# Issue order of the q, k and v loads around the DMA transposes, in a retention layer followed by a bilinear feed-forward layer

## The chip, the cores and the metric

The kernel runs on one core of one Trainium2 chip. The metric is the device time of one execution in microseconds, as the median of several runs. The engines are TensorE (PE in the profile, with its weight loads as PEld), VectorE (DVE), ScalarE (ACT), GpSimd (POOL) and SyncE (SP), which here only issues DMA transfers.

## What is computed

Four sequences of 768 steps, 8 heads of 64. Each head keeps a state of 64 x 64 that decays by a factor of its own; the output of that recurrence is the input x of a feed-forward layer with two products that are multiplied element by element.

```python
gamma = 1.0 - 2.0 ** (-5.0 - np.arange(H))
for t in range(S):
    state = gamma * state + einsum('bhd,bhe->bhde', k[:, :, t], v[:, :, t])
    y[:, :, t] = 1/sqrt(D) * einsum('bhd,bhde->bhe', q[:, :, t], state)
x = y.transpose(0, 2, 1, 3).reshape(3072, 512)
out = ((x @ w_a) * (x @ w_b)) @ w_out          # d_ff = 1536
```

## The kernel before

**Slots and blocks.** The 3072 rows are 24 slots of 128, six to a sequence; a sequence is worked on slot by slot, with the state carried along. The feed-forward layer runs over seven blocks of 4, 2, 2, 2, 2, 4 and 8 slots (`TILES`), named J = 0 to 6. While PE works on the feed-forward products of one block, the recurrence of the slots that come next is put between them (in block 3, slots 8 and 9, that of slots 10 to 13). The whole order is written out by hand at the end of the kernel (lines 888 to 1071), and `seq` chains the instructions of each engine in the order of the program, so no scheduler changes it.

**From load to scores.** Slots 0 to 5 are loaded in pairs and transposed on PE. From slot 6 on, a slot t goes this way:

1. SP loads k, q and v from DRAM (`load_slot`, lines 106 to 120). k and v come one slot at a time (256 KB each), into halves of a tile that two slots share. q comes for two slots at once (`load_two`, 512 KB), with the even one of them. The pool `raw` has three buffers for each of k, q and v.
2. POOL scales k and q with the decay tables into the bf16 tile `kqb` (`scaled`, line 283, 1.04 us each) and casts v (line 242); for slots 12 to 19, ACT casts v (`v_cast`).
3. SP issues a DMA transpose of `kqb` into `kqT` (`flip`, line 303). It waits for POOL's scaling of that slot.
4. PE reads `kqT` in `turn(new, old)` (lines 392 to 411): scores of the pair `new` (line 330), and output of the pair `old`. Scores of a slot need the transposes of both slots of its pair.

`casts(t)` (lines 290 to 298) does 2 and 3 for one slot and then issues the loads of slot t + 2. `casts_two(6)` (lines 307 to 315) does 2 and 3 for slots 6 and 7 and then issues the loads of slots 8 and 9 (`load_slots`).

**SP's queue.** SP works through its instructions in order; one that waits (a transpose for POOL, a store for its result) holds all behind it. The first loads of the program are a list, `LOADS` (line 21): pairs 0 and 1, weights, pair 2, output weights, and at its end `s6`, the loads of slots 6 and 7. All that is left of it after the first six entries is issued at line 923. Behind it come the transposes of 6 and 7, then the loads of 8 and 9, then for each slot its transpose and the loads of two slots later, with finished rows of the output (line 551) between them.

**Two slots that differ.** For t = 14 and t = 18 (`LATE_Q`, line 20), q is not issued with the even slot. It is issued at the head of the loads of slot 15 and slot 19, which stand in the queue behind the transposes of 13 and 17.

**Sums ahead of the products.** The output product of blocks 1 to 6 works with seven products in place of eight (`Group`, `single`), and needs sums and differences of parts of ht, the product of the two branches: tiles hs 1 to 4 (`hsum`, `hsums`, line 575). For blocks 2, 3 and 4, POOL makes them, between the casts: the difference hs 3 over all of ft 0 to 5, then hs 2, 1 and 4 in two halves, the first of which needs ft up to 8 and the second up to 11. In `single(J)`, PE uses hs 3 first, then hs 2, hs 1 and hs 4, with products of block J + 1 between them. In `big()` (block 6), POOL makes sums of the weights (`weight_pieces`) and then products into ht, which take part in the rotation of the buffers that DVE writes.

**Lines of the order that matter here.** `casts_two(6)` stands at line 981, `casts(8)` at 990, `casts(9)` at 998. `casts(12)` to `casts(14)` stand at 1009 to 1015 and `casts(16)` to `casts(18)` at 1030 to 1039, with `hsums(2, ...)`, `hsum(3, ...)`, `hsums(3, ...)` and `hsum(4, ...)` between them, all of them on POOL in that order.

Of the kernel before, what the change touches and what calls it, by code (L numbers as in the profile page):

```python
# [16 lines left out]
PAIRS = 3  # L17


LATE_Q = {14, 18}  # L20
LOADS = "p0 p1 w0 w1 a1 b1 a2 k2 q2 b2 v2 o0 o1 o2 o3 o4 o5 s6".split()


@with_exitstack
def kernel(
# [69 lines left out]
    def seq(bi):  # L95
        ins = bi.ins
        prev = last.get(ins.engine)
        if prev is not None:
            tc.add_manual_dep(ins, prev.name, nosync, reason="program order")
        last[ins.engine] = ins  # L100
        return bi
# [3 lines left out]

    def load_slot(t, names="kqv"):
        b, ci = divmod(t, NCH)
        if t - 1 in LATE_Q:
            load_two("q", q, b, ci // 2, t - 1)
        for nm in names:  # L110
            src = {"k": k, "q": q, "v": v}[nm]
            if nm == "q":
                if t % 2 == 0 and t not in LATE_Q:
                    load_two(nm, src, b, ci // 2, t)
                continue
            if t % 2 == 0:
                whole[nm] = raw.tile([P, 2, H, D], F32, tag=nm + "f", name=nm + "f")
            raws[nm, t] = whole[nm][:, t % 2]
            s = src[b, :, ci * P : (ci + 1) * P, :].rearrange("h p d -> p h d")
            seq(nc.sync.dma_start(out=raws[nm, t], in_=s))  # L120

    def load_slots(t):
        for u, names in ((t, "kq"), (t + 1, "k"), (t, "v"), (t + 1, "v")):
            load_slot(u, names)

    def load_two(nm, src, b, u, t):
        f = raw.tile([P, H, 2, D], F32, tag=nm + "f", name=nm + "f")
        s = src[b, :, 2 * u * P : 2 * (u + 1) * P, :].rearrange("h (p two) d -> p h two d", two=2)
        seq(nc.sync.dma_start(out=f, in_=s))  # L129
        for par in range(2):  # L130
            raws[nm, t + par] = f[:, :, par, :]
# [5 lines left out]
    def load_wide(nm, n):  # L137
        src = {"a": moe_w_a, "b": moe_w_b}[nm]
        for i in range(2):
            st = wstage.tile([P, 2, 2 * WC], F32, tag="w", name="wst" + nm)  # L140
            s = src[2 * i * P : 2 * (i + 1) * P, 2 * n * WC : 2 * (n + 1) * WC]
            seq(nc.sync.dma_start(out=st, in_=s.rearrange("(c p) f -> p c f", p=P)))
            wst[nm, n, i] = st
# [13 lines left out]

    pending = list(LOADS)

    def issue_loads(n):  # L160
        for _ in range(min(n, len(pending))):
            what = pending.pop(0)
            n = int(what[1:])
            if what[0] in "ab":
                load_wide(what[0], n)
            elif what[0] in "kqv":
                load_two(what[0], {"k": k, "q": q, "v": v}[what[0]], 0, n, 2 * n)
            else:
                {"p": load_pair, "s": load_slots, "w": load_w, "o": load_o}[what[0]](n)


    kqb = {}
    kqb = {}
    issue_loads(6)
    zero = osbp.tile([P, DM], F32, tag="osb", name="zero")
    seq(nc.vector.memset(zero, 0.0))
# [61 lines left out]
    def cast(engine, dst, src):  # L238
        if engine is nc.scalar:
            seq(nc.scalar.copy(dst, src))  # L240
        else:
            seq(engine.tensor_copy(dst, src))  # L242
# [29 lines left out]
    def scaled(eng, t, i):  # L272
        tab = tabs[0] if i else tabs[1 if t < 2 * PAIRS else 2]
        dst, src, tab = kqb[t][:, i], raws["kq"[i], t], tab[:, t % NCH]
        if t < 2 * PAIRS:
            dst, src = (x.rearrange("p (hp r) d -> p hp r d", r=2) if x is src else x
                        for x in (dst, src))
            tab = tab.rearrange("p (hp r) o -> p hp r o", r=2).to_broadcast([P, HP, 2, D])
        else:
            dst = dst.rearrange("p hp r d -> p r hp d")  # L280
            src = src.rearrange("p (r hp) d -> p r hp d", r=2)
            tab = tab.rearrange("p (r hp) o -> p r hp o", r=2).to_broadcast([P, 2, HP, D])
        seq(eng.tensor_tensor(dst, src, tab, op=ALU.mult))  # L283

    def new_nat(t):
        kqb[t] = nat.tile([P, 2, HP, 2, D], BF16, tag="kqb", name="kqb")
        kb[t], qb[t] = kqb[t][:, 0], kqb[t][:, 1]
        vb[t] = nat.tile([P, H, D], BF16, tag="vb", name="vb")

    def casts(t):  # L290
        new_nat(t)
        scaled(nc.gpsimd, t, 0)
        scaled(nc.gpsimd, t, 1)
        if t not in range(12, 20):
            cast(nc.gpsimd, vb[t], raws["v", t])
        flip(t)
        if t + 2 < NSLOT:
            load_slot(t + 2)

    def flip(t):  # L300
        if t % 2 == 0:
            kqT[t // 2] = tra.tile([P, 2, 2, HP, P], BF16, tag="kqT", name="kqT", bufs=3)
        seq(nc.sync.dma_start_transpose(
            out=kqT[t // 2][:, t % 2].rearrange("p a b c -> p (a b) c"),
            in_=kqb[t].rearrange("p a hp r d -> p (a hp r d)")))

    def casts_two(t):
        for u in (t, t + 1):
            new_nat(u)
            scaled(nc.gpsimd, u, 0)  # L310
            scaled(nc.gpsimd, u, 1)
            flip(u)
        for u in (t, t + 1):
            cast(nc.gpsimd, vb[u], raws["v", u])
        load_slots(t + 2)

    def half(i):
        return slice(64 * i, 64 * i + 64)
# [602 lines left out]
    update2(1, 1)  # L921
    ffn_g(0, 0, 0, W2)
    issue_loads(100)
    cast_w(1, parts=2)
    ffn_a(0, 0, W2, 2 * W2)
# [53 lines left out]
    for ft in range(NFT):  # L979
        ffn_ab(1, ft)  # L980
    casts_two(6)
    ffn_out(0, 0, 0)
    weight_sum(3)
# [118 lines left out]
```

## Time and profile before

| | |
|---|---|
| median of 3 runs | 222.21 us (222.01 to 222.92) |
| the profiled execution: its time | 222.79 us |
| the profiled execution: its span | 221.1 us |
| HBM read, written | 28.31 MB, 6.29 MB |
| share of the DMA engines taken by SP's queue | 75.8% |

The span is the time from the first to the last instruction that the profile shows. In a timeline, a row has the start in us, the duration in us, engine, line, operation and tiles, and the number of instructions that are merged into it; in brackets stands how long the engine was idle before it and what ended the idle time. On SP's queue (SPq) the duration is that of issuing a transfer, not of the transfer. A row of DMA issues has the tile, the count, the size and the median time from issue to landing.

### The profile page before, as it was taken

The numbers are of one execution on the slowest core, as the hardware profiler recorded it, in microseconds if no ns is written. First come the engines' busy times: TensorE is split into PE (matmuls) and PEld (weight loads), VectorE is DVE, ScalarE is ACT, GpSimd is POOL, SyncE is SP. The second block draws the span as 40 slices with busy tenths as digits, with TensorE's granted clock in tenths as the row PEclk, the third lists the DMA queues.
The fourth block names the chain that finished last, engine by engine and source line by source line (L and its number), as shares of the span: only waits on it lengthen the run. The fifth ranks groups of instructions, "written<-read, shape, count | busy, mean of one in ns | idle before, by whom it ended". The sixth has DMA issues, their size and how long they took to land.

```text
span 221.1 us, 5640 instructions
## 1 busy us (share of the span) xinstructions
PE 212.3 (96%) x2242; PEld 143.3 (65%) x2242; DVE 138.0 (62%) x254; ACT 99.3 (45%) x217; POOL 141.2 (64%) x163
## 2 busy tenths in 40 slices
PE   6789999999999999998999999999999999999994
PEld 2467445687468888887888565456865444448883
DVE  3776356846393463774377246986595777789642
ACT  3255325342243453453475345445545656542331
POOL 5265876775364659349782976999999996520000
PEclk9999999999999999999999999999999999999999
DMA  6999999998999999869999999990022000000054
GB/s 167 290 323 367 382 313 361 374 235 152 251 193 291 207 236 220 180 143 190 271 181 247 225 147 227 246 175 3 4 80 110 0 1 3 0 0 1 27 190 166
DMA packets 85146, 39.68 MB, mean 179 GB/s; under 512 B 57472, under 2 KB 78848, under 8 KB 85120
## 3 DMA queue, kind: packets, MB, share of 16 engines
q1 hardware_dynamic: 84976, 39.26, 75.8%
q8 instruction: 17, 0.28, 0.6%
q10 hardware_dynamic: 144, 0.07, 0.1%
q14 instruction: 9, 0.07, 0.1%
HBM read 28.31 MB, written 6.29 MB: 157 GB/s over the span
## 4 chain that ended last, share of the span: by engine, by line
PE 87%; SPq 4%; DMA 4%; POOL 2%; issue 1%; DVE 1%; ACT 0%; DVEq 0%
PE a L525 19%; PE g L537 18%; PE mA L641 12%; PE uA L781 8%; PE mB L641 6%; PE o L562 5%; PE uB L781 4%; DMA wstb<-in_moe_w_b_dram 4%; SPq L129 3%; PE mC L641 3%; PE at L330 2%; PE y L378 2%; PE uC L781 2%; PE st L348 2%; POOL hs L575 2%; PE ka L840 2%
## 5 line engine op out<-in xcount | busy, mean ns | idle before, releaser
L539 DVE TENSOR_TENSOR ht<-g,asb 128x256 bf16<-128x256 f32 (+1 forms) x74 | 36.9, 502 | 38.4 <-PE g L537 33.8
L525 PE MATMUL a<-xt,wa_bf 128*128 128x256 bf16 (+1 forms) x296 | 52.4, 305 | 0.2
L537 PE MATMUL g<-xt,wb_bf 128*128 128x256 bf16 (+1 forms) x296 | 52.2, 304 | 0.2 <-POOL wb_bf L242 0.2
L528 ACT CAST asb<-a 128x256 bf16<-128x256 f32 (+1 forms) x74 | 32.3, 437 | 39.0 <-PE a L525 36.6
L537 PEld LDWEIGHTS <-wb_bf 128*128 128x128 bf16 x296 | 28.6, 98 | 12.8 <-POOL wb_bf L242 0.3
L525 PEld LDWEIGHTS <-wa_bf 128*128 128x128 bf16 x296 | 27.9, 98 | 12.5 <-POOL wa_bf L242 0.4
L283 POOL TENSOR_TENSOR kqb<-kf,ktab 128x512 bf16<-128x512 f32 x22 | 23.0, 1051 | 16.6 <-DMA kf<-in_k_dram 14.9
L283 POOL TENSOR_TENSOR kqb<-qf,qtab 128x512 bf16<-128x512 f32 x18 | 19.0, 1053 | 12.8 <-DMA qf<-in_q_dram 12.8
L641 PEld LDWEIGHTS <-hs 128*128 128x128 bf16 x240 | 23.1, 98 | 5.6 <-POOL hs L575 1.7
L787 ACT COPY snap<-uA 128x512 f32<-128x512 f32 x30 | 16.7, 588 | 13.1 <-PE uA L781 13.1
L336 DVE TENSOR_TENSOR aT<-at,mask 128x512 bf16<-128x512 f32 x36 | 22.3, 681 | 0.3
L648 ACT COPY snaps<-mA 128x256 f32<-128x256 f32 x30 | 11.2, 374 | 21.2 <-PE mA L641 21.2
L641 PEld LDWEIGHTS <-ht 128*128 128x128 bf16 x180 | 17.5, 98 | 2.8
L575 POOL TENSOR_TENSOR hs<-ht,hs 128x384 bf16<-128x384 bf16 (+1 forms) x17 | 16.5, 982 | 2.5 <-DVE ht L539 2.5
L641 PE MATMUL mA<-wsum,hs 128*128 128x256 bf16 x120 | 16.1, 273 | 1.1 <-POOL hs L575 1.1
L575 POOL TENSOR_TENSOR ht<-gsb,asb 128x512 bf16<-128x512 bf16 x12 | 13.5, 1159 | 4.5 <-DVE gsb L575 4.5
L242 POOL CAST vb<-vf 128x512 bf16<-128x512 f32 x16 | 10.1, 645 | 8.4 <-DMA vf<-in_v_dram 8.2
L575 DVE TENSOR_TENSOR osb<-mB,snaps 128x256 f32<-128x256 f32 x20 | 8.4, 422 | 9.1 <-PE mB L641 4.7
L575 POOL TENSOR_TENSOR hs<-ht 128x384 bf16<-128x384 bf16 (+2 forms) x12 | 13.8, 1153 | 0.0
L389 ACT CAST xt<-y 128x512 bf16<-128x512 f32 x18 | 9.7, 589 | 2.3 <-PE y L378 2.2
L562 PE MATMUL o<-wo_bf,ht 128*128 128x512 bf16 x48 | 10.7, 379 | 0.0
L575 DVE TENSOR_TENSOR gsb<-uB,snap 128x512 bf16<-128x512 f32 x10 | 6.9, 685 | 5.4 <-ACT snap L787 2.6
(104 smaller groups left out, 325.9 us busy)
## 6 DMA issues: line engine op xcount, KB each, us to landing
qf<-in_q_dram SPq DMA_DIRECT2D x12, 512.0 KB, 5.9
out_dram<-osb SPq DMA_DIRECT2D x21, 256.0 KB, 4.2
kf<-in_k_dram SPq DMA_DIRECT2D x18, 256.0 KB, 4.6
vf<-in_v_dram SPq DMA_DIRECT2D x18, 256.0 KB, 5.3
wsta<-in_moe_w_a_dram SPq DMA_DIRECT2D x6, 512.0 KB, 7.9
wstb<-in_moe_w_b_dram SPq DMA_DIRECT2D x6, 512.0 KB, 8.2
wsto<-in_moe_w_out_dram SPq DMA_DIRECT2D x6, 512.0 KB, 8.7
kf<-in_k_dram SPq DMA_DIRECT2D x3, 512.0 KB, 7.2
```

The costliest lines, as they stand in the source:

```text
L283: seq(eng.tensor_tensor(dst, src, tab, op=ALU.mult))
L336: seq(nc.vector.tensor_tensor(aT[t][:, r], at[r], mask.to_broadcast([P, HP, P]), op=ALU.mult))
L525: seq(nc.tensor.matmul(a, wa_bf[:, kt, fs], xcols(J, kt, c0, c1), start=(kt == 0), stop=(kt == KT - 1)))
L528: seq(nc.scalar.copy(asb, a))
L537: seq(nc.tensor.matmul(g, wb_bf[:, kt, fs], xcols(J, kt, c0, c1), start=(kt == 0), stop=(kt == KT - 1)))
L539: seq(nc.vector.tensor_tensor(ht[J][:, ft, c0:c1], g, asbs.pop((J, ft, c0)), op=ALU.mult))
L562: seq(nc.tensor.matmul(o, ht[J][:, ft, i * P : (i + 1) * P], wo_bf[:, ft], start=(ft == 0), stop=(ft == NFT - 1), skip_group_check=True))
L575: seq(eng.tensor_tensor(dst, x, y, op=op))
L641: seq(nc.tensor.matmul(m, w, right[:, j], start=(first and j == 0), stop=(j == NP - 1), skip_group_check=True))
L648: seq(nc.scalar.copy(self.snaps[:, n], self.bank["A"]))
L781: seq(nc.tensor.matmul(m, w, right[:, k], start=(first and k == 0), stop=(k == 1), skip_group_check=True))
L787: seq(nc.scalar.copy(self.snaps[n], self.bank["A"]))
```

## The change

Three edits. `t8` is put at the end of `LOADS`: the loads of slot 8 (k, q of 8 and 9, v) are issued right behind those of slots 6 and 7, ahead of their transposes. `casts_two` issues the loads of slot 9 alone behind the transposes (k and v). `LATE_Q` goes: q of 14 and 15 is issued with slot 14 between its k and v, ahead of the transpose of 13, and q of 18 and 19 with slot 18, ahead of the transpose of 17. The instructions of PE, DVE, ACT and POOL are the same ones in the same order.

```diff
-LATE_Q = {14, 18}
-LOADS = "p0 p1 w0 w1 a1 b1 a2 k2 q2 b2 v2 o0 o1 o2 o3 o4 o5 s6".split()
+LOADS = "p0 p1 w0 w1 a1 b1 a2 k2 q2 b2 v2 o0 o1 o2 o3 o4 o5 s6 t8".split()
...
     def load_slot(t, names="kqv"):
         b, ci = divmod(t, NCH)
-        if t - 1 in LATE_Q:
-            load_two("q", q, b, ci // 2, t - 1)
         for nm in names:
             src = {"k": k, "q": q, "v": v}[nm]
             if nm == "q":
-                if t % 2 == 0 and t not in LATE_Q:
+                if t % 2 == 0:
                     load_two(nm, src, b, ci // 2, t)
                 continue
...
-                {"p": load_pair, "s": load_slots, "w": load_w, "o": load_o}[what[0]](n)
+                {"p": load_pair, "s": load_slots, "t": load_slot, "w": load_w, "o": load_o}[what[0]](n)
...
         for u in (t, t + 1):
             cast(nc.gpsimd, vb[u], raws["v", u])
-        load_slots(t + 2)
+        load_slot(t + 3)
```

## The prediction

> **What bounds the kernel now.** I read the page first, then the list of what TensorE waited for to find the places, then the timelines of PE, GpSimd (POOL), VectorE (DVE) and SyncE's queue (SP) around those waits, and last the landing time of single transfers.
>
> ```profile
> span 221.1 us, 5640 instructions
> ...
> PE 212.3 (96%) x2242; PEld 143.3 (65%) x2242; DVE 138.0 (62%) x254; ACT 99.3 (45%) x217; POOL 141.2 (64%) x163
> ```
>
> PE is busy for 212.3 of 221.1 us. A change that only moves loads can win nothing but PE's waits. What one costs is read from the starts of neighbouring groups on PE's timeline, since the pipeline has to fill again after a wait:
>
> ```profile
> 103.70 0.49 PE L641 MATMUL mA<-wsum,hs 128*128 128x256 bf16 x3
> 105.26 0.50 PE L641 MATMUL mA<-wsum,hs 128*128 128x256 bf16 x3 [1.07 <-POOL hs L575]
> 105.60 0.60 PE L525 MATMUL a<-xt,wa_bf 128*128 128x256 bf16 x4
> ...
> 106.47 0.82 PE L641 MATMUL mA<-wsum,hs 128*128 128x256 bf16 x6
> 107.13 0.60 PE L525 MATMUL a<-xt,wa_bf 128*128 128x256 bf16 x4
> ...
> 124.46 1.02 PE L641 MATMUL mA<-wsum,hs 128*128 128x256 bf16 x6
> 125.33 1.03 PE L525 MATMUL a<-xt,wa_bf 128*128 128x512 bf16 x4
> ```
>
> Six undisturbed mA matmuls take 107.13 - 106.47 = 0.66 us until the next group starts. In single(3) the six on hs 2 stop after three, until POOL's hs is there, and take 105.60 - 103.70 = 1.90: 1.24 us lost. In single(4) the same product takes 125.33 - 124.46 = 0.87: 0.21 lost. The third place is found in the chain of waits, in big():
>
> ```profile
> 173.96 0.86 PE uA L781 x4
> ...
> 176.98 0.86 PE uA L781 x4
> ...
> 180.46 0.86 PE uA L781 x4
> ```
>
> The period of two units is 176.98 - 173.96 = 3.02 us, and the next one takes 3.48: 0.46 lost. In all 1.24 + 0.21 + 0.46 = 1.91 us, and that is the most that I can see to win.
>
> Why POOL was late at the first two places, and what else it waits for:
>
> ```profile
> 57.19 1.04 POOL L283 TENSOR_TENSOR kqb<-kf,ktab 128x512 bf16<-128x512 f32 x1 [3.84 <-DMA kf<-in_k_dram]
> ...
> 80.27 0.91 POOL L575 TENSOR_TENSOR hs<-ht,hs 128x384 bf16<-128x384 bf16 x1 [2.55 <-DVE ht L539]
> ...
> 90.46 1.04 POOL L283 TENSOR_TENSOR kqb<-kf,ktab 128x512 bf16<-128x512 f32 x1 [0.93 <-DMA kf<-in_k_dram]
> 97.08 1.04 POOL L283 TENSOR_TENSOR kqb<-qf,qtab 128x512 bf16<-128x512 f32 x1 [5.58 <-DMA qf<-in_q_dram]
> ...
> 103.42 1.78 POOL L575 TENSOR_TENSOR hs<-ht,hs 128x384 bf16<-128x384 bf16 x2
> ...
> 120.41 1.04 POOL L283 TENSOR_TENSOR kqb<-qf,qtab 128x512 bf16<-128x512 f32 x1 [5.06 <-DMA qf<-in_q_dram]
> ...
> 123.15 1.78 POOL L575 TENSOR_TENSOR hs<-ht,hs 128x384 bf16<-128x384 bf16 x2
> ...
> 134.47 1.04 POOL L283 TENSOR_TENSOR kqb<-kf,ktab 128x512 bf16<-128x512 f32 x1 [3.25 <-DMA kf<-in_k_dram]
> ```
>
> The two longest waits, 5.58 us at q of slot 14 and 5.06 at q of slot 18, are the two loads that the change moves. From 97.08 POOL works without a gap to 103.42 + 1.78 = 105.20, and PE goes on right there. So the chain is: q of 14 lands late, 8.12 us of POOL work behind it are late, PE stands.
>
> **The change part by part.** No instruction of PE, DVE, ACT or POOL is added, removed or moved; the same DMAs with the same bytes are issued by SP in another order. So every term is a matter of when something lands.
>
> (1) *q of 14, two places forward in SP's queue.* It passes v of 14 and the transpose of slot 13; both of these now have its 512 KB ahead of them. For k and v of 15, which stood behind it already, nothing is added.
>
> ```profile
> 86.87 0.63 SPq L120 DMA_DIRECT2D vf<-in_v_dram  x1
> 89.56 1.24 SPq L303 DMA_TRANSPOSE kqT<-kqb  x1
> 90.84 0.58 SPq L129 DMA_DIRECT2D qf<-in_q_dram  x1
> ```
>
> q is issued where v of 14 stood, at 86.87 and not at 90.84, 3.97 us earlier. It took 97.08 - 90.84 = 6.2 us to land; other landing times, each from a view of one issue (in this order: q of 10, which like the new q of 14 stands between its k and v; the transposes of slot 7 and of slot 11):
>
> ```profile
> qf<-in_q_dram SPq DMA_DIRECT2D x1, 512.0 KB, 6.6
> ...
> kqT<-kqb SPq DMA_TRANSPOSE x1, 3.2
> ...
> kqT<-kqb SPq DMA_TRANSPOSE x1, 7.3
> ```
>
> With 6.6 it lands at 93.5. POOL then meets DVE: hs 3 of block 3 needs the product ht of ft 5, and the second half of hs 2 that of ft 11. DVE's rows:
>
> ```profile
> 61.08 0.42 DVE L242 CAST gst<-st 128x256 bf16<-128x256 f32 x1 [3.78 <-PE st L348]
> ...
> 94.12 1.07 DVE L539 TENSOR_TENSOR ht<-g,asb 128x256 bf16<-128x256 f32 x3
> ...
> 101.13 0.42 DVE L539 TENSOR_TENSOR ht<-g,asb 128x256 bf16<-128x256 f32 x1 [0.30 <-PE g L537]
> ...
> 121.27 0.42 DVE L539 TENSOR_TENSOR ht<-g,asb 128x256 bf16<-128x256 f32 x1
> ...
> 178.09 0.69 DVE L575 TENSOR_TENSOR gsb<-uB,snap 128x512 bf16<-128x512 f32 x1 [2.11 <-POOL ht L575]
> ```
>
> ht of ft 4, 5 and 6 are the three of 94.12, so ft 5 is done at about 94.9. From q's end (98.12) to 105.20 POOL needed 7.08: 94.9 + 7.08 = 102.0. The last step needs ft 11 of 101.13 + 0.42 = 101.55 and takes 0.9, so 102.5. PE needs it at 103.70 + half of 0.66 = 104.0. The whole 1.24 goes, with 1.5 us to spare. k of 15, which the chain needs too, is issued in the place that q leaves, with one load fewer between it and the transpose. Bounds of this term: 1.24, and 0 if q of 14 or k of 15 lands no sooner than POOL took it in the profile.
>
> (2) *q of 18, in the same way.* It is now ahead of the transpose of slot 17:
>
> ```profile
> 112.71 2.48 SPq L303 DMA_TRANSPOSE kqT<-kqb  x1
> 115.25 0.57 SPq L129 DMA_DIRECT2D qf<-in_q_dram  x1
> ```
>
> It leaves at least 115.25 - 112.71 = 2.5 us earlier, more since POOL, which releases the transposes, runs ahead. The second half of hs 2 of block 4 waits for ft 11, 121.27 + 0.42 = 121.7, now 1.24 earlier with PE: 120.4, against a start of 123.15 + 0.89 = 124.0. The 0.21 goes; 0 is the other end.
>
> (3) *What POOL gains behind it.* POOL runs 124.0 - 120.4 = 3.6 us earlier from there. The scaling of slot 19 releases its transpose, and k of 21 stands behind that in SP's queue, so the 134.47, at which POOL's last stretch begins, moves with it. At 178.09 DVE waits 2.11 us for an ht product of that stretch, and PE's third loss follows from it. PE comes 1.45 earlier, POOL 3.6: the 2.1 us between them cover the wait, and of PE's 0.46 all goes. If POOL did not move at all there, PE would run into the wait 1.45 earlier and lose 0.46 + 1.45. So the bounds of this term are +0.46 and -1.45; I take +0.46, because what starts the stretch hangs on POOL itself.
>
> (4) *Slot 8 ahead of the transposes of 6 and 7.* POOL's wait of 3.84 at 57.19 goes, since k of 8 is issued right behind v of 7:
>
> ```profile
> 45.61 2.90 SPq L120 DMA_DIRECT2D vf<-in_v_dram  x2
> ```
>
> that is at 48.5. PE gets nothing of it: at 80.27 POOL waits 2.55 us for DVE, which hangs on PE, so whatever POOL gains before is lost there. The price lies with the transposes of 6 and 7, which have 1 MB ahead of them. PE's scores of 6 and 7, of 12 and 13 and of 16 and 17, each of which needs both transposes of its pair, and the issue of the transposes of 6 and 7:
>
> ```profile
> 60.97 0.64 PE L330 MATMUL at<-kqT 64*64 64x128 bf16 x32
> ...
> 97.54 0.64 PE L330 MATMUL at<-kqT 64*64 64x128 bf16 x32
> ...
> 118.31 0.73 PE L330 MATMUL at<-kqT 64*64 64x128 bf16 x32
> ```
>
> ```profile
> 49.85 3.64 SPq L303 DMA_TRANSPOSE kqT<-kqb  x2
> ```
>
> The transpose of 7 is issued when POOL has scaled slot 7, as before (49.85 + 3.64 less an issue of 1.24, about 52.3), and landed 3.2 later, at 55.5. The slowest transpose, that of 11, also right behind a slot's k, q and v, took 7.3: 52.3 + 7.3 = 59.6, still 1.4 us ahead of 60.97. The transpose of 13, behind q of 14, would land at 89.56 + 7.3 = 96.9, 0.7 ahead of 97.54. I take nothing for either; should that of 7 back up behind that of 6 by another 3.2, it is 1.8 us of stall, the far end.
>
> One thing more moves: POOL now scales slot 8 between 53 and 57, when DVE makes the weight sums, and where POOL had been idle. Such a meeting shows later in the profile, in the same hs difference with a POOL cast beside it and without:
>
> ```profile
> 64.47 0.85 DVE L575 TENSOR_TENSOR hs<-ht,hs 128x768 bf16<-128x768 bf16 x1
> ...
> 65.71 0.54 DVE L575 TENSOR_TENSOR hs<-ht,hs 128x768 bf16<-128x768 bf16 x1
> ```
>
> 0.31 us for one; eight weight sums make 2.5 at most, under the 3.78 that DVE is idle before 61.08. Cost nothing; without that cover it would be 2.5. (The Trainium skill, SBUF — State Buffer, "Who interferes with whom", is harsher: a VectorE instruction with two SBUF inputs and a GpSimd one that reads SBUF exclude each other for the whole instruction. By it DVE would lose up to the three POOL operations, an estimated 2.7 us, which the idle time still holds; the 0.85 agrees in kind, not in full size.)
>
> **The sum.** 1.24 + 0.21 + 0.46 = 1.91 us off the profiled execution's 222.79: 220.88. That execution lies 0.58 above the median of the runs (222.21); the same step below it gives 220.3.
>
> **The rivals.**
>
> *Given back at 178.* POOL's last stretch starts with a wait for a transfer (134.47). If k of 21 is late for DMA's own reasons, term (3) is -1.45 and takes back all of (1) and (2): 222.79, at the median 222.2. For it: the wait at 134.47 is one for the transfer, and what POOL does not win there DVE waits for at 178.09. Against: k of 21 is issued only after POOL's own scaling of 19.
>
> *The load does not come sooner.* q of 14 lands at about 97 because the DMA rings, not the issue, are the limit; then nothing changes, 222.2. For: POOL waited 0.93 for k of 14 as well. Against: 6.6, the slowest q row, still gives 93.5.
>
> *Slower: the transpose of 17 comes late at 118.31.* q of 18 stands ahead of it. It is issued at 112.71 at the latest; with the 7.3 of the transpose of 11 it lands at 120.0. PE stands 1.7 us behind the old timeline, whatever it won before: 222.79 + 1.7 = 224.5, at the median 223.9. It decides from a landing after 118.3 - 1.24 = 117.1 on and makes the kernel slower from 118.3 on. For: from issue to use it has 118.31 - 112.71 = 5.6 us, the transpose of 7 has 8.7 and that of 13 has 8.0. Against: POOL should issue it some 3 us sooner. [...]
>
> **How the numbers follow.** Forecast as summed: 0.62. Given back: 0.12. No sooner: 0.07. Slower: 0.19. A measurement of this kernel can tell about 0.5% (1.1 us) from no change. Faster by more than that (below 221.1) holds in the forecast except when term (1) comes only in part: 0.60. Within: 0.20, the two middle rivals and that rest. Slower: 0.20. The forecast's own range is 219.8 to 221.0, its top being term (1) alone (222.21 - 1.24). For 8 in 10 I go up to 223.0, through the two middle rivals and a part of the slower one.
>
> **What would show it.** Right: POOL's wait for q of 14 falls from 5.58 to under 3, no PE wait for hs remains in single(3) and single(4), POOL's k of 21 starts near 131, and the period around 178 is 3.02. Step (4) is right if PE has no gap at the scores of 6 and 7 and POOL still meets DVE near 80.3. Wrong: a PE gap ahead of any scores on kqT, above all in turn(16, 14) or turn(6); a period longer than 3.48 near 178; q of 14 taken by POOL after 95.9, from where (104.0 - 8.12) it costs PE again.

## The result and the profile after

| | before | after |
|---|---|---|
| median of 7 runs each, side by side | 222.88 us | 220.99 us |
| lowest and highest of these runs | 222.01 and 223.35 | 220.85 and 221.85 |
| the profiled execution: its time | 222.79 us | 221.23 us |
| the profiled execution: its span | 221.1 us | 219.5 us |

The ratio of after to before is 0.9928, with a 95% interval of 0.9906 to 0.9949: the changed kernel is faster by 0.5 to 0.9%. The two profiled executions differ by 222.79 - 221.23 = 1.56 us. The engines' line of the page of after:

```profile
PE 212.4 (97%) x2242; PEld 143.6 (65%) x2242; DVE 139.1 (63%) x254; ACT 99.3 (45%) x217; POOL 142.1 (65%) x163
```

PE's work is the same to 0.1 us; its waits became fewer. The list of what TensorE waited for (in all, times, longest, in us) is the shortest way to see which:

```profile
PE idle L506 <- DVE zero L173: 1.5, 1, 1.5
PE tp L431 <- DVE kqb L280: 1.4, 3, 0.9
PE idle L506 <- ACT kqT L237: 0.4, 1, 0.4
PE a L522 <- DVE ht L536: 0.2, 1, 0.2
```

The first three are in the start-up, before any load that the change touches is used. The last row is new. Two rows of the list of before are gone, the waits in single(3) and in big():

```profile
PE mA L641 <- POOL hs L575: 1.1, 1, 1.1
...
PE uB L781 <- DVE asb L575: 0.3, 1, 0.3
```

(The 0.21 us of single(4) have no row in that list.)

PE's timeline of after, at the places of before and at the new wait:

```profile
103.80 0.82 PE L638 MATMUL mA<-wsum,hs 128*128 128x256 bf16 x6
104.45 0.60 PE L522 MATMUL a<-xt,wa_bf 128*128 128x256 bf16 x4
...
117.16 0.73 PE L327 MATMUL at<-kqT 64*64 64x128 bf16 x32
...
123.32 0.82 PE L638 MATMUL mA<-wsum,hs 128*128 128x256 bf16 x6
123.97 1.03 PE L522 MATMUL a<-xt,wa_bf 128*128 128x512 bf16 x4
...
142.76 0.62 PE L375 MATMUL y<-aT,vb 128*64 128x128 bf16 x16
143.57 1.02 PE L522 MATMUL a<-xt,wa_bf 128*128 128x512 bf16 x4 [0.19 <-DVE ht L536]
...
177.87 0.59 PE L778 MATMUL uB<-xs,wsa 128*128 128x512 bf16 x2
```

The six matmuls on hs 2 run through: 104.45 - 103.80 = 0.65 us in single(3) and 123.97 - 123.32 = 0.65 in single(4). The chain of waits has the period of big() back at 175.87 - 172.85 = 178.89 - 175.87 = 3.02:

```profile
172.85 0.86 PE uA L778 x4
...
175.87 0.86 PE uA L778 x4
...
178.89 0.86 PE uA L778 x4
```

All that PE won or lost is read from the start of the same group in both traces. In this table each number is such a start in us; the columns are the product behind hs 2 in single(3), the scores of slots 16 and 17, the product behind hs 2 in single(4), the product behind turn(20, 18), and the products into uB behind the third loss. The rows of the experiments are used further down.

| | single(3) | scores 16, 17 | single(4) | behind turn(20, 18) | uB in big() | span |
|---|---|---|---|---|---|---|
| before | 105.60 | 118.31 | 125.33 | 144.66 | 179.44 | 221.1 |
| after | 104.45 | 117.16 | 123.97 | 143.57 | 177.87 | 219.5 |
| q14_only | 104.22 | 116.93 | 123.74 | 143.08 | 177.39 | 219.0 |
| both_q | 104.39 | 117.10 | 123.91 | 143.36 | 177.66 | 219.3 |
| q18_only | 106.04 | 119.39 | 126.11 | 145.87 | 180.17 | 221.8 |
| slot8_only | 105.24 | 117.95 | 124.76 | 144.10 | 178.41 | 220.0 |
| k21_late | 104.43 | 117.14 | 123.95 | 143.29 | 177.83 | 219.5 |
| sum_to_pool | 104.52 | 117.23 | 124.05 | 143.38 | 177.69 | 219.3 |
| l19_ahead | 104.38 | 118.79 | 125.51 | 144.92 | 179.21 | 220.9 |
| three_ahead | 104.34 | 118.86 | 125.58 | 144.92 | 179.23 | 220.9 |
| k21_behind_k22 | 104.32 | 117.03 | 123.85 | 143.18 | 179.32 | 220.9 |
| k21_behind_q22 | 104.30 | 117.01 | 123.83 | 143.16 | 181.26 | 222.9 |

After against before: -1.15, -1.15, -1.36, -1.09, -1.57. The hs 2 of single(3) itself begins 0.10 later than before (103.80 for 103.70, from the start-up), so the first wait gave 1.25; the second gave 0.21; behind turn(20, 18) 0.27 is lost; the third place gave 0.48. Sum: -0.10 + 1.25 + 0.21 - 0.27 + 0.48 = 1.57, against 1.56 measured.

How POOL got there, on its timeline of after (in brackets the wait ahead of the row):

```profile
80.37 0.92 POOL L572 TENSOR_TENSOR hs<-ht,hs 128x384 bf16<-128x384 bf16 x1 [2.64 <-DVE ht L536]
...
92.52 1.04 POOL L280 TENSOR_TENSOR kqb<-qf,qtab 128x512 bf16<-128x512 f32 x1 [0.76 <-DMA qf<-in_q_dram]
...
101.74 0.91 POOL L572 TENSOR_TENSOR hs<-ht,hs 128x384 bf16<-128x384 bf16 x1 [0.18 <-DVE ht L536]
...
114.44 1.04 POOL L280 TENSOR_TENSOR kqb<-qf,qtab 128x512 bf16<-128x512 f32 x1 [0.23 <-DMA qf<-in_q_dram]
...
130.27 1.04 POOL L280 TENSOR_TENSOR kqb<-kf,ktab 128x512 bf16<-128x512 f32 x1 [2.40 <-DMA kf<-in_k_dram]
```

The waits for q of 14 and of 18 fell from 5.58 and 5.06 us to 0.76 and 0.23. The second half of hs 2 of block 3 is done at 101.74 + 0.91 = 102.65, and now ends a wait for DVE, not a backlog of POOL. SP's queue of after, q of 14, v of 18 and the transpose of slot 17, and the landing of the first and the last of these from a view of that one issue (us in the last column):

```profile
86.96 0.62 SPq L126 DMA_DIRECT2D qf<-in_q_dram  x1
...
109.40 1.69 SPq L117 DMA_DIRECT2D vf<-in_v_dram  x1
111.19 3.25 SPq L300 DMA_TRANSPOSE kqT<-kqb  x1
```

```profile
qf<-in_q_dram SPq DMA_DIRECT2D x1, 512.0 KB, 5.5
...
kqT<-kqb SPq DMA_TRANSPOSE x1, 5.4
```

q of 14 landed at 92.5. The transpose of 17 landed at 111.19 + 5.4 = 116.6; PE asks for it at 117.16. This is the narrowest place that the change leaves: 0.6 us. POOL's scaling of slot 17 did not hold that transpose:

```profile
109.56 1.04 POOL L280 TENSOR_TENSOR kqb<-qf,qtab 128x512 bf16<-128x512 f32 x1
```

It was done at 109.56 + 1.04 = 110.60, but SP was issuing v of 18 until 109.40 + 1.69 = 111.09. (Before, POOL was done at 112.68 and the transpose was issued at 112.71.)

The new loss of 0.27 us. Before and after, DVE's timeline ahead of the product behind turn(20, 18):

```profile
142.09 0.63 DVE L575 TENSOR_TENSOR hs<-ht 128x512 bf16<-128x512 bf16 x1
142.65 1.26 DVE L575 TENSOR_TENSOR hs<-ht,hs 128x512 bf16<-128x512 bf16 x1
143.83 0.68 DVE L539 TENSOR_TENSOR ht<-g,asb 128x512 bf16<-128x512 f32 x1
```

```profile
140.74 0.99 DVE L572 TENSOR_TENSOR hs<-ht 128x512 bf16<-128x512 bf16 x1
141.65 1.26 DVE L572 TENSOR_TENSOR hs<-ht,hs 128x512 bf16<-128x512 bf16 x1
142.84 0.68 DVE L536 TENSOR_TENSOR ht<-g,asb 128x512 bf16<-128x512 f32 x1
```

Before, ht is done at 144.51 and PE goes on at 144.66, just in time. After, everything comes earlier, but DVE's first sum takes 0.99 us in place of 0.63. ht is done at 143.52. PE's y group starts at 142.76; before, the next group followed 0.55 us behind that start (144.11 and 144.66), so PE could have gone on at 143.31. POOL, now earlier too, scales slots at that time, and both engines read SBUF; the last section has the rows.

### The profile page after: what moved, and what is told of

It reads as the page before. It is cut to its first block, busy times and chain, and to the rows that moved or that the text cites. A ratio compares the mean times of both kernels' runs of the same rounds, so it can differ in the third digit from the quotient of the medians.

```text
span 219.5 us, 5638 instructions
## 1 busy us (share of the span) xinstructions
PE 212.4 (97%) x2242; PEld 143.6 (65%) x2242; DVE 139.1 (63%) x254; ACT 99.3 (45%) x217; POOL 142.1 (65%) x163
## 4 chain that ended last, share of the span: by engine, by line
PE 89%; SPq 3%; DMA 3%; issue 1%; DVE 1%; POOL 0%; ACT 0%; DVEq 0%
PE a L522 19%; PE g L534 19%; PE mA L638 12%; PE uA L778 8%; PE mB L638 6%; PE o L559 5%; PE uB L778 4%; SPq L126 3%; DMA wsta<-in_moe_w_a_dram 3%; PE mC L638 3%; PE at L327 2%; PE uC L778 2%; PE y L375 2%; PE ka L837 2%; PE kb L837 2%; PE st L345 1%
```

## The experiments

The experiments ran in three sets, each beside the kernel before, whose medians were 222.44 us (23 runs; the first set, q14_only to both_q), 222.36 (26; the second, k21_late, l19_ahead, three_ahead and sum_to_pool) and 222.42 (26; the third, the two k21_behind kernels and q14_and_sum). A ratio is to the kernel before of the same set. Each trace is of one execution.

### Which of the three edits does it

**Only q of 14 moved** (q14_only), on the kernel before:

```diff
-LATE_Q = {14, 18}
+LATE_Q = {18}
```

> The kernel before with only the first moved load: q of 14 is issued with slot 14, q of 18 still with slot 19, slot 8 as before. Theory (each of PE's losses has its own cause): the loss in single(3) goes (1.24 us); in single(4) POOL still waits for q of 18, so the 0.21 there stays or grows a little, because PE comes 1.24 earlier and the load only some 1.5 earlier; the loss near 178 stays near 0.46. About 1.2 us faster than before, POOL's wait for q of 14 under 1.5 us, the one for q of 18 still over 3 us. Rival (given back): POOL's last stretch stays where it was at 134.5, PE comes to it 1.2 earlier, and the loss near 178 grows to about 1.7; then no gain over 0.3 us.

220.93 us, ratio 0.9932 (0.9917 to 0.9946): one moved load is the whole gain. Against before, the table has -1.38, -1.38, -1.59, -1.58, -2.05. The wait in single(3) went, as expected, but so did the other two, which should have stayed. q of 18 still stands behind the transpose of 17 here. SP's row and POOL's:

```profile
111.40 0.58 SPq L129 DMA_DIRECT2D qf<-in_q_dram  x1
```

```profile
116.82 1.04 POOL L283 TENSOR_TENSOR kqb<-qf,qtab 128x512 bf16<-128x512 f32 x1 [2.86 <-DMA qf<-in_q_dram]
...
130.80 1.04 POOL L283 TENSOR_TENSOR kqb<-kf,ktab 128x512 bf16<-128x512 f32 x1 [2.55 <-DMA kf<-in_k_dram]
```

Unmoved, q of 18 is issued at 111.40 and not at 115.25, and POOL takes it at 116.82 and not at 120.41. What holds it in the queue is the transpose in front of it, and that waits for POOL, which q of 14 has made earlier. k of 21 comes at 130.80, nearly where after has it (130.27).

**Only q of 18 moved** (q18_only):

```diff
-LATE_Q = {14, 18}
+LATE_Q = {14}
```

> The kernel before with only the second moved load: q of 18 is issued with slot 18, q of 14 still with slot 15. Theory: the loss of 1.24 in single(3) stays; the 0.21 in single(4) goes; POOL's k of 21 starts some 3.5 us earlier than 134.5, and with it the 0.46 near 178 goes. About 0.6 us faster than before. Rival (transpose of 17 late behind q of 18, POOL not ahead this time): a gap of up to 1 us ahead of the scores of 16 and 17, and the kernel is about 0.3 us slower than before.

223.08 us, ratio 1.0028 (1.0013 to 1.0044): slower by about 0.6 us. This is the "slower" rival of the prediction, seen at its place: SP's row, the landing of that transpose, PE's row, and what the weight loads of PE waited for between 117 and 121.

```profile
113.19 4.21 SPq L303 DMA_TRANSPOSE kqT<-kqb  x1
```

```profile
kqT<-kqb SPq DMA_TRANSPOSE x1, 6.2
```

```profile
119.39 0.64 PE L330 MATMUL at<-kqT 64*64 64x128 bf16 x32 [0.57 <-DVE ht L539]
```

```profile
PEld L330 <- DMA kqT<-kqb: 0.9, 1, 0.9
```

113.19 + 6.2 = 119.39, the very time at which PE starts the scores. PE's row names DVE as the releaser, but the landing and the weight loads, which go ahead of the matmuls, name the transfer. From single(3) on PE was 0.44 late, and at the scores it is 1.08 late: 0.64 us are the price of q of 18 ahead of the transpose, where POOL has not been made earlier.

The two later losses went, as expected. From the scores to the product behind hs 2 in single(4) PE takes 126.11 - 119.39 = 6.72 us (before 7.02, after 6.81), and from the product behind turn(20, 18) to uB 180.17 - 145.87 = 34.30 (before 34.78, after 34.30). Between the two, DVE's sums cost 0.43 us (145.87 - 126.11 = 19.76, before 19.33), the loss that after has as 0.27.

**Only slot 8 moved** (slot8_only), the `LOADS` and `casts_two` parts of the change on the kernel before:

```diff
-LOADS = "p0 p1 w0 w1 a1 b1 a2 k2 q2 b2 v2 o0 o1 o2 o3 o4 o5 s6".split()
+LOADS = "p0 p1 w0 w1 a1 b1 a2 k2 q2 b2 v2 o0 o1 o2 o3 o4 o5 s6 t8".split()
...
-        load_slots(t + 2)
+        load_slot(t + 3)
```

> The kernel before with only the loads of slot 8 ahead of the transposes of 6 and 7. Theory: no change (within 0.3 us): POOL takes slot 8 some 4 us earlier but meets VectorE at 80.3 as before, and the three losses of PE stay 1.24, 0.21 and 0.46. Rival: it does carry a part of the gain, and the kernel is 0.5 us or more faster.

222.51 us, ratio 0.9996 (0.997 to 1.0023): no difference. Its profiled execution was its fastest, 221.76. The loss in single(3) is still there, but smaller. Three profiled executions with q of 14 in its old place show how it depends on when POOL takes q of 14 (the columns are readings of POOL's timeline, and of PE's: start of the group behind hs 2, less the start of hs 2, less 0.66):

| | POOL takes q of 14 | lost in single(3) |
|---|---|---|
| slot8_only | 96.73 | 105.24 - 103.67 - 0.66 = 0.91 |
| before | 97.08 | 105.60 - 103.70 - 0.66 = 1.24 |
| q18_only | 97.53 | 106.04 - 103.68 - 0.66 = 1.70 |

0.8 us later at q is 0.8 us more at PE. The same row of SP's queue (issued at 90.79 to 90.84 in all three) gives another time from one execution to the next, and it goes straight into the kernel's time.

Against the expectation, the two later losses are not in this execution, though neither q moved: 124.76 - 117.95 = 6.81 us from the scores to single(4), and 178.41 - 144.10 = 34.31 from turn(20, 18) to uB, both as in after. POOL took q of 14 0.35 us earlier than in before, q of 18 1.19 earlier (119.22) and k of 21 1.07 earlier (133.40). So these two losses hang on about 1 us of POOL's lateness, and which of them an execution of before has can differ from one to the next.

**Both q moved, slot 8 not** (both_q): `LATE_Q = set()`.

> The kernel before with both moved q loads, slot 8 as before. Theory: all of the change's gain, 1.5 to 1.9 us faster than before, with PE's losses in single(3), single(4) and near 178 gone and the new 0.27 us ahead of the products after the scores of 20 and 21 as in the changed kernel. Rival: slot 8 is needed for the gain, and less than 1 us comes.

220.94 us, ratio 0.994 (0.9922 to 0.9958): as after (220.99) and as q of 14 alone (220.93). With q of 14 moved, q of 18 may stand on either side of the transpose.

### What could take the gain back

**k of 21 later** (k21_late), on the changed kernel: loads of slot 21 issued with slot 20's, behind the transpose of 20.

```diff
+        if t == 20:
+            load_slot(21)
-        if t + 2 < NSLOT:
+        if t + 2 < NSLOT and t != 19:
             load_slot(t + 2)
```

> The changed kernel, but k and v of slot 21 are issued behind the transpose of 20, not behind that of 19. Theory (PE's loss near 178 is POOL's lateness against PE): POOL's k of 21 starts near 135 in place of 130.3, so POOL is about 5 us later and PE is not; the period near 178, 3.02 us in the changed kernel, loses about 2 to 2.5 us, and the time is back at the kernel before (within 0.7 us of it). Rival: POOL's stretch has room by then, and the loss is at most the 0.46 of before; then the kernel is still over 1 us faster than before.

221.55 us, ratio 0.9964 (0.9943 to 0.9985), 0.81 us below before (after's ratio was 0.9928; the profiled execution: 221.22). This lies between the theory and the rival. POOL took k of 21 at

```profile
132.92 1.04 POOL L280 TENSOR_TENSOR kqb<-kf,ktab 128x512 bf16<-128x512 f32 x1 [4.81 <-DMA kf<-in_k_dram]
```

2.65 us later than after, not the some 5 that the expectation rests on: the transpose of 20 is issued soon behind that of 19. Between the product behind turn(20, 18) and uB, PE gained 1.61 - 1.37 = 0.24 us over before; after gained 1.57 - 1.09 = 0.48 there. So half of the third loss is back. By the prediction's own rule (the loss of 0.46, less what POOL is earlier than before, plus what PE is earlier) it should be 0.46 - (134.47 - 132.92) + 1.37 = 0.28, and 0.48 - 0.24 = 0.24 is found. The rule held; the move was too small to test the rival.

**k and v of 21 behind k of 22** (k21_behind_k22) and **behind k and q of 22** (k21_behind_q22), on the changed kernel, to move POOL's stretch further:

```diff
-        if t + 2 < NSLOT:
+        if t == 20:
...
+            load_slot(22, "k")
...
+            load_slot(21)
...
+            load_slot(22, "qv")
+        elif t + 2 < NSLOT and t != 19:
             load_slot(t + 2)
```

(the second has "kq" and "v" in place of "k" and "qv").

> The changed kernel with k and v of 21 behind k of 22, all behind the transpose of 20 (in k21_late they stood ahead of k of 22, POOL took k of 21 at 132.9, and PE lost 0.24 near 178). Theory: PE's loss there is 0.46 plus what POOL's start of k of 21 moves later than 134.47, plus what PE's position moves earlier. POOL's start comes near 134.0 and PE is 1.4 ahead of the kernel before, so the loss is near 1.4 us, and most of the gain is gone: about 222.0. Rival: the 0.24 does not grow with POOL's lateness; then under 0.5 us is lost and the time stays near 221.3.

> As k21_behind_k22, with q of 22 (512 KB) ahead of k and v of 21 as well. Theory, by the same sum: POOL's start near 135.9, PE 1.4 ahead, a loss near 178 of about 3.2 us, so this kernel is slower than before by 1.5 to 2 us; a gap ahead of the scores of 20 and 21 may add a few tenths, since the transpose of 21 waits for POOL as well. Rival: under 1 us is lost, and the kernel is no slower than before.

222.67 us, ratio 1.0007 (0.9985 to 1.0029), and 224.62 us, ratio 1.009 (1.0057 to 1.0123). In the first, POOL's row and what TensorE waited for:

```profile
134.49 1.04 POOL L280 TENSOR_TENSOR kqb<-kf,ktab 128x512 bf16<-128x512 f32 x1 [6.71 <-DMA kf<-in_k_dram]
```

```profile
PE at L335 <- DMA kqT<-kqb: 0.9, 1, 0.9
...
PE uB L786 <- DVE asb L580: 0.3, 1, 0.3
PE mA L646 <- POOL hs L580: 0.2, 1, 0.2
```

With POOL's stretch where before had it (134.49 for 134.47), the whole gain is given back: at uB PE is at 179.32, before at 179.44. The total is what the prediction's rival "given back at 178" says. Its place is not: the first 0.96 us go at the scores of slots 22 and 23 (PE 1.48 ahead of before at 143.18, 0.52 ahead at those scores, 149.42 for 149.94), because a late k of 21 makes POOL late for slots 22 and 23 too, and with it their transposes (issued from 143.77 on, before from 143.66); some 0.4 more go at hs sums near 155, and only the old 0.46 in big(). In the second, POOL starts at 135.98 and the wait at those scores is

```profile
PE at L335 <- DMA kqT<-kqb: 2.2, 1, 2.2
```

and 1.46 us more are lost right behind it (PE 0.82 behind before at 150.76, 2.28 at 155.11). No wait of PE stands there: its matmuls are slow. The view of one stretch (after the length, the busy time of PE, PEld, DVE, ACT and POOL, then the granted clock, the DMA share and GB/s):

```profile
151.00:155.00 4.00, 4.00 (x82) 3.13 (x71) 2.48 (x4) 1.82 (x4) 4.00 (x5) 0.57 0.02 4
```

The granted clock was 0.57 in it, 0.50 from 152.0 to 154.0, and 1.00 from 140 to 150 and from 156 on. It fell right behind the wait of 2.2 us; behind those of 0.9, 1.6 and 1.7 us in the other traces of this section it stayed at 1.00. Four of the seven executions have a mean clock of 0.992 and took 224.62 to 225.11 us; the other three, at 0.997 and 1.00, took 223.94 to 224.31. So the kernel is slower by 2.2 us, near the 1.5 to 2 expected, but by a gap at scores and a slower clock, where a loss near 178 was forecast. PE is then so late that big() has no loss of its own: 2.28 behind before at 155 (155.11 for 152.83), 1.82 at uB, the difference being the 0.46 that before loses there.

**Slot 19 ahead of the transpose of 17** (l19_ahead), on the changed kernel: the 512 KB of k and v of slot 19 issued ahead of that transpose, not behind it.

```diff
+        if t == 17:
+            load_slot(19)
         flip(t)
-        if t + 2 < NSLOT:
+        if t + 2 < NSLOT and t != 17:
             load_slot(t + 2)
```

> The changed kernel with k and v of slot 19 (512 KB) issued ahead of the transpose of 17 as well. Theory (that transpose is the tightest, and it cannot land before what stands ahead of it): it lands at about 118.8, not 116.6, PE wants it at 117.2, so a gap of 1.5 us or more ahead of the scores of 16 and 17, and the kernel gives back most of its gain (within 0.6 us of before). Rival (the transpose's landing depends on when POOL releases it, not on the loads ahead): no gap there, and the kernel stays over 1.2 us faster than before.

222.45 us, ratio 0.9997 (0.9978 to 1.0015): the gain is gone. What TensorE waited for has the wait that the prediction's rival "slower" names, at its place:

```profile
PE at L329 <- DMA kqT<-kqb: 1.6, 1, 1.6
```

The transpose is issued at 113.51, 2.3 us later than after, and PE goes from 1.22 ahead of before to 0.48 behind. POOL had scaled slot 17 by 110.51, as early as in after (110.60), so the loads ahead did it, and mostly through SP: it was issuing them until 111.79 + 1.62 = 113.41. Then the transpose lands behind the load ahead of it. In five traces it came 0.8 to 0.9 us behind that load (load and transpose of 17: 116.3 and 117.2 in before, 115.7 and 116.6 in after, 114.0 and 114.9 in q14_only, 118.5 and 119.4 in q18_only, 117.9 and 118.7 here).

**All later loads three slots ahead** (three_ahead), on the changed kernel: `t9` at the end of `LOADS`, `load_slot(t + 4)` in `casts_two`, `load_slot(t + 3)` in `casts`.

> The changed kernel with every later load one slot earlier still: slot 9 too ahead of the transposes of 6 and 7, then each slot's loads three slots ahead. Theory: PE has nothing left to win from loads; the transpose of 7 lands some 2 us later than in the changed kernel (near 60) and PE wants it at 61, so no gap there; the transpose of 17 has 512 KB right ahead of it and not 1 MB, so its margin grows. Time within 0.4 us of the changed kernel. Rival: the transposes of 6 and 7 come after 61, a gap of 1 us or more there, and the kernel loses it.

221.03 us, ratio 0.9948 (0.9923 to 0.9974). Eight of ten executions lie between 220.88 and 221.25, two at 222.60 and 222.84. The profile happens to be of the one of 222.60:

```profile
PE at L327 <- DMA kqT<-kqb: 1.7, 1, 1.7
```

It is the wait for slots 16 and 17 again: the transpose of 17 issued at 112.99 and landed 5.8 later, at 118.8. No wait at the scores of 6 and 7, though both slots 8 and 9 now stand ahead of their transposes. My expectation of a wider margin at 17 was wrong: issued 1.8 us later than in after (111.19), the transpose has less. POOL had scaled slot 17 already by 108.28; SP had the transpose of 16 (issued from 108.57 to 111.62) and two loads to issue first. An order that is mostly as good falls over this now and then; of the other nine executions there is no trace.

### The new loss behind turn(20, 18)

**One hs sum moved from DVE to POOL** (sum_to_pool), on the changed kernel:

```diff
-    WHEN = {5: ["302"], 6: ["324"], 7: ["346", "202"], 8: ["102", "402"], 9: ["224", "124"],
+    WHEN = {5: ["302"], 6: ["324"], 7: ["346"], 8: ["202", "102", "402"], 9: ["224", "124"],
```

> The changed kernel with one of VectorE's sums for block 5 (the first third of hs 2, at ft 7) given to POOL at ft 8. Theory (the 0.27 us that PE loses after the scores of 20 and 21 comes from VectorE's hs operations, lengthened beside POOL's scalings: 0.99 and 1.26 us in place of 0.63): with one of them gone VectorE is in time, the 0.27 is gone, and POOL, 1.15 later, is still early enough near 178. About 0.2 to 0.3 us faster than the changed kernel. Rival (PE waits there for something else, or POOL's later end costs it near 178): the 0.27 stays, or a loss of 0.3 or more appears near 178.

220.85 us, ratio 0.9913 (0.9881 to 0.9944). DVE now has one sum in that place, and PE goes on at 143.38, 0.55 behind the start of its y group at 142.83, without a wait:

```profile
140.82 0.67 DVE L572 TENSOR_TENSOR hs<-ht 128x512 bf16<-128x512 bf16 x1
```

That DVE's lateness is the cause of the 0.27 is shown; its worth in the time, 220.99 against 220.85 in different sets, is less than the runs can tell. The same edit with q of 14 alone (q14_and_sum) was to be the best version:

> The kernel before with only q of 14 moved, and the first third of hs 2 of block 5 given to POOL as in sum_to_pool. Theory: none of PE's losses is left (1.24, 0.21, 0.46 and the new 0.27 all absent), so it is as fast as the fastest of the others, 220.6 to 220.9, about 0.7% faster than before, and its runs lie within 0.4 us. Rival: POOL, with that sum more and q of 18 still late, comes late near 178, and a loss of 0.3 us or more shows there.

220.92 us, ratio 0.9937 (0.9912 to 0.9963); eleven of twelve executions between 220.73 and 221.56, one at 223.27. No better than q of 14 alone, in whose trace the loss did not occur anyway (its y group at 142.53, the product at 143.08). The trace is of the execution of 223.27, and in it not all losses are gone: against q14_only PE is 1.40 us late from the start-up on, loses 0.63 more near 155 (a wait of 0.5 for POOL's hs) and 0.49 in big() (a period of 180.94 - 177.43 = 3.51), with k of 21 taken by POOL at 134.03. So this one execution has what the rival describes; whether the eleven faster ones had none of it is not shown. No version beats the changed kernel by more than its runs spread.

## Why the prediction was right, and where it was not

**The bound.** Right: three waits of PE made up what could be won, and they went. 1.24, 0.21 and 0.46 were foreseen; 1.25, 0.21 and 0.48 came.

**Step (1), q of 14.** Right: landing by 93.5 (92.5), hs 2 done at 102.5 (102.65), the whole wait in single(3) gone. The rival that it would land no sooner is out. Two readings beside it were wrong without harm. The 6.6 us of q of 10 is the slowest q row only from slot 8 on; q of 6 took 10.6. And k of 15 was not issued in the place that q left: it was issued at 92.26, later than before (91.47), since the transpose of 13 took 2.56 us to issue in place of 1.24. POOL waited 0.23 us for it, which the 1.5 us to spare covered.

**Steps (2) and (3), q of 18 and what POOL gains behind it.** The sizes are right and k of 21 came near 131 (130.27), but the cause is only one of several that do. The prediction put the 0.21 and the 0.46 down to q of 18's own move. Alone, that move does take both away (q18_only), at a price of 0.64 us at the scores; but q14_only has both gains without it, and in the trace of slot8_only both losses are missing with neither q moved. What failed is the sentence that made q of 18's place in the queue the reason for POOL's second long wait. Its place mattered only as long as POOL was late. The prediction had both halves of this in hand, that POOL releases the transposes and that POOL would run ahead, and did not carry it to q of 18 unmoved.

**Step (4), slot 8.** Right, and shown by slot8_only: nothing. POOL met DVE at 80.37 (80.3 foreseen). The contention with the weight sums came as well. DVE's first and last row of the eight, and its idle time behind them:

```profile
53.58 1.34 DVE L572 TENSOR_TENSOR wsum<-wo_bf 128x768 bf16<-128x768 bf16 x2
...
57.97 1.01 DVE L572 TENSOR_TENSOR wsum<-wo_bf,wsum 128x768 bf16<-128x768 bf16 x2
...
61.18 0.42 DVE L239 CAST gst<-st 128x256 bf16<-128x256 f32 x1 [2.20 <-PE st L345]
```

The eight end 57.97 + 1.01 - 53.58 = 5.40 us after they began, and DVE's idle time fell from 3.78 to 2.20: 1.58 us, of at most 2.5 foreseen, all of it hidden. (The Trainium skill, SBUF — State Buffer, "Who interferes with whom", gave an estimated 2.7 as the most. The rows agree with it in kind: the three sums that met POOL's scaling of k, its scaling of q and its cast ended 0.4 us behind them (54.45 for 54.03, 56.69 for 56.28 and 57.58 for 57.17, from the start and duration of the single instructions). Less was lost since POOL had begun k 0.59 us ahead of DVE, and had to wait for DVE itself: its other two took 1.17 and 0.94 us in place of 1.04 and 0.61.) The transpose of 7 landed at 58.0, 3.1 us ahead of PE's scores.

**The rival "slower".** Not what happened, but the real danger. "Some 3 us sooner" was too much: the transpose of 17 was issued 112.71 - 111.19 = 1.5 us sooner, while PE asked for it 1.15 sooner, and it took 5.4 us in place of 4.5 with q of 18 ahead of it. POOL had slot 17 scaled 2.1 us sooner (110.60 for 112.68), and SP, still busy issuing the loads put ahead, was 0.6 us behind that; in q14_only, with q of 18 left behind the transpose, it was issued at 109.89, 2.8 us sooner. The prediction had no term for SP's own time to issue the load. In after it landed at 116.6, half a microsecond before the 117.1 that the prediction named as the point of decision. q18_only, l19_ahead and three_ahead each passed such a point and lost 0.64 to 1.8 us.

**The rival "given back".** It did not happen because k of 21 followed POOL by 4.2 us, more than PE's gain. Where k of 21 was held back, the gain went as the rival says, but mostly at the scores of 22 and 23, a place that the prediction did not look at.

**The predicted time, 220.3 us, was 0.7 low,** and the measured one lies at the very top of the forecast's own range (221.0). The miss has two steps. First the sum: 1.91 us between the profiled executions, where 1.56 came. The terms held; the sum lacked the 0.27 us of DVE's sums beside POOL's scalings, which the prediction had as a mechanism in (4) but sought only near 53 us, and 0.10 in the start-up. Second, "the same step below it": 0.58 was taken off since the profiled execution of before lay that far above the median of three runs. After's lay 0.24 above its own median, so 0.34 of it was not there: 0.35 + 0.34 = 0.69. The 0.58 also came from a median of only three runs: the same execution of before lies 0.09 below the median of the seven runs beside after, and 0.35 to 0.43 above those of the three larger sets. Since before's seven runs lay high, it is luck that the medians of the seven differ by 1.89 us, nearly the 1.91 of the sum. The step assumes that the surplus of an execution survives the change. The table of three executions shows that the time of a kernel with q of 14 in its old place moves by the very wait that the change removes, so some of that surplus may have been counted twice; that it was this wait in the three unprofiled runs is only argued.

## What to carry to other kernels

A load is late for all that queues behind its taker: follow the chain from the load through the engine that takes it to the next transfers which that engine releases, and repair its first link alone before moving the others, since a later late load may be only its echo. For each transfer that a load is moved past, write down issue, landing and use, and call the change safe only if the gap between landing and use is wider than the landing time varies from run to run. Count the queue's own time to issue what is put ahead, too. When part of the spread of a kernel's runs comes from the wait that is to be removed, leave the distance of the profiled execution from the median out of the sum.

## What was not expected of the hardware

The time of one and the same DVE sum (two bf16 inputs in SBUF, 128x512) ran from 0.41 to 1.26 us, depending on which of DVE and POOL began first. DVE's and POOL's rows in q14_only:

```profile
141.06 0.41 DVE L575 TENSOR_TENSOR hs<-ht,hs 128x512 bf16<-128x512 bf16 x1
```

```profile
141.08 1.29 POOL L283 TENSOR_TENSOR kqb<-kf,ktab 128x512 bf16<-128x512 f32 x1 [0.23 <-DMA kf<-in_k_dram]
```

and POOL's in after:

```profile
140.41 1.04 POOL L280 TENSOR_TENSOR kqb<-kf,ktab 128x512 bf16<-128x512 f32 x1
141.41 1.22 POOL L280 TENSOR_TENSOR kqb<-qf,qtab 128x512 bf16<-128x512 f32 x1
```

Where DVE starts 0.02 us ahead, it keeps its 0.41 and POOL's scaling takes 1.29 in place of 1.04. Where POOL starts at 141.41 and DVE at 141.65, DVE's takes 1.26. The sum that starts second ends 0.28 us behind POOL's scaling: (141.65 + 1.26) - (141.41 + 1.22) = 0.28, and for the sum ahead of it (140.74 + 0.99) - (140.41 + 1.04) = 0.28. So in these rows it waits for the whole scaling. (The Trainium skill, in the section on SBUF named above, says that a VectorE instruction with two SBUF inputs contends with a GpSimd one that reads SBUF; these rows agree.) So a kernel that is brought forward by a microsecond in one place can meet such a pair in another order, and win or lose a quarter of a microsecond that no term of a sum over waits contains.

The landing of a 512 KB q load differs between executions by more than the effect of some edits: of the loads of q of 14 in the old place, issued within 0.05 us of one another, POOL took the data at 96.73, 97.08 and 97.53 (the orders of the last two are the same up to there; the first has slot 8 moved, some 40 us earlier). Behind a wait of 2.2 us for a transpose, TensorE had a mean granted clock of 0.57 for 4 us (k21_behind_q22), and 1.46 us more were lost there.

Executions of before ranged over 220.95 to 223.73 us in one set of 26, while five of six of both_q and all six of q14_only lay within 0.4 us.
